# Attention scores by 64x64 matmuls on the four quarters of the array, two units at a time

## The chip, the cores and the metric

One core of one Trainium2 chip runs the whole program in one launch. Its engines are TensorE (PE: matmuls; PEld: its loads of weights), VectorE (DVE), ScalarE (ACT), GpSimd (POOL) and SyncE (SP), which issues most DMAs. The metric is the device time of one execution in microseconds, as the median of several runs.

## What is computed

Three layers, one after another, all in float32 accuracy. Only the first is touched:

```python
scores = scale * np.matmul(q, k.transpose(0, 1, 3, 2))   # q, k, v: 4 x 8 heads x 576 x 64
rel = pos[:, None] - pos[None, :]
mask = (rel >= 0) & (rel < 64)                           # causal, a window of 64
scores = np.where(mask, scores, -1e9)
attn = softmax(scores); x = np.matmul(attn, v)
```

The second layer is `h = x @ w_in`, a rational function of `h`, and `@ w_out` (512 to 2048 to 512, for 2304 tokens). The third sends each token to one of eight experts (512 to 1024 to 512) and scales what comes back.

## The kernel before

The 2304 tokens are cut into nine blocks of 256 (`TB`), and a block's attention into four units, each a pair of heads: 36 units (`NUNIT`), number `n` = 4 u + c. A block holds four pieces of 64 queries (`W`); a piece of queries sees its own 64 keys and the 64 before them, so its scores are 64 x 128 for each head.

A unit goes through four steps. `at_T(n)` turns q and k by four transposes into the PSUM tile `tq`; ScalarE or VectorE copies k's half into `kT[c]` and q's half, scaled, in two copies of 64 x 256 into `qbd`, a tile cleared once in which each piece has the two heads on the diagonal. `at_QK(n)` makes the scores: one matmul for each piece, contracting 128 rows (two heads of 64) and giving 128 rows (head, query) by 128 keys in the tile `sc`, one PSUM bank. VectorE adds the mask and takes the least value, ScalarE the exponential, and the rows are divided by their sums; all four pieces are in the tile `ms`. `at_PT(n)` turns `ms` into PSUM (`pp`) and back. `at_PV(n)` multiplies by v: matmuls of 128 rows by 64 columns, the two heads on the two column halves of the array, into `xp`; from block 3 (`NG`) on it takes two units at once.

An fp32 matmul is two records in the trace, one of fp32r (`h`, `y`, `lt`) is one.

The second layer runs in steps `s` of one block and two pieces of `w_in`; `h` is its first product (each 24 matmuls of 128x128 by 256), `y` its second (12 by 512, four steps later). The attention's work is cut into half-steps (`evs`, two for each unit) and dealt out between those steps by `pace(s)`, which has a block's attention done (`need`) when the second layer comes to it. `ORDER` gives the order of every engine's work in the first twelve steps (`S_TAPE`) by hand, with the units 0 to 12 in it; instructions from there bear the line L125 in the trace. What follows is placed by a planner and bears the line L97. `in_turn` keeps a group of matmuls behind the last such group. The weights are split into high and low parts in the start (`convert`, VectorE's tile `cp`).

Of the kernel before, what the change touches and what calls it, by code (L numbers as in the profile page):

```python
# [23 lines left out]
NQ, TA, VU = 2, 2, 2  # L24
# [107 lines left out]
def kernel(  # L132
# [56 lines left out]
    sizes = dict(cs=C_QC + 1, mb=128, co=6, OH=2 * E, idt=3 * NTILE, npre=E, pre=2 * NPRE, ei=2 * (NSLOT + 1), nsl=1,  # L189
                 CNT=E, CN2=E, tri=64, one=64, sg=24, qbd=NQ * 512, kT=NP * (W + TB))  # L190
# [14 lines left out]
    qbd = [cols["qbd"][:, i * 512:(i + 1) * 512].rearrange("p (b q) -> p b q", b=4) for i in range(NQ)]  # L205
# [197 lines left out]
    def at_T(n):  # L403
        nc.mark()
        u, c = divmod(n, NP)
        tq = pt([128, 2, 2, 128], "tq")
        cc = 2 * (c % 2)
        for a, src in ((0, k_t[n // 2]), (1, q_t[n // 2])):
            for r in range(2):
                nc.tensor.transpose(tq[:, a, r, :], src[:, r, cc:cc + 2, :].rearrange("p h d -> p (h d)"), ident)  # L410
        if u:
            e = pick(D=dve(W, True), A=act(W), G=0.2)
            nc.either(e if e == "G" else "D", G=lambda: nc.gpsimd.tensor_copy(out=kT[c][:, :W], in_=kT[c][:, TB:]),
                      D=lambda: nc.vector.tensor_copy(out=kT[c][:, :W], in_=kT[c][:, TB:]))
        evac(kT[c][:, W:], tq[:, 0].rearrange("d r p -> d (r p)"), TB)
        for hh in range(2):
            lo = 64 * hh
            evac(qbd[n % NQ][lo:lo + 64, :, lo:lo + 64],
                 tq[lo:lo + 64, 1].rearrange("d r (b p) -> d (r b) p", b=2), 256, -scale)

    def spans(nk):
        a = 0
        while a < 4:
            b = a
            while b < 4 and nk[b] == nk[a]:
                b += 1
            yield a, b, nk[a]
            a = b

    def mask(u, i, w):  # L430
        m = mb if u and (4 * u + i) % BPS == 0 else cs[:, C_MASK:C_MASK + 128]
        return m[:, 128 - w:]

    def at_QK(n):
        nc.mark()
        u, c = divmod(n, NP)
        sc = pt([128, 4, 128], "sc")
        ms = t2([128, 4, 128], "ms")
        mn = sm.tile([128, 4], F32, tag="mn", name="mn")
        rs = sm.tile([128, 4], F32, tag="sg", name="rs")  # L440
        nk = []
        kt = kT[c]
        for i in range(4):
            w = W if u + i == 0 else 2 * W
            mm(sc[:, i, :w], qbd[n % NQ][:, i, :], kt[:, i * W + 2 * W - w:(i + 2) * W], True, True)
            nk.append(w)
        for i in range(4):
            charge("D", dve(128))
            nc.vector.tensor_tensor_reduce(
                out=ms[:, i, :nk[i]], in0=sc[:, i, :nk[i]], in1=mask(u, i, nk[i]),  # L450
                scale=1.0, scalar=3.0e38, op0=ALU.add, op1=ALU.min, accum_out=mn[:, i:i + 1],
            )
        for i in range(4):
            charge("A", act(128))
            nc.scalar.activation(out=ms[:, i, :nk[i]], in_=ms[:, i, :nk[i]], func=AF.Exp,
                                 scale=-1.0, bias=mn[:, i:i + 1], accum_out=sg[n % 3][:, i, 0:1])
# [3 lines left out]
        for a, b, w in spans(nk):  # L460
            arith(ms[:, a:b, :w], ms[:, a:b, :w], bc(rs[:, a:b], [128, b - a, w]), ALU.mult, (b - a) * w)
        P_t[n] = (ms, nk)

    def at_PT(n):
        nc.mark()
        ms, nk = P_t.pop(n)
        pp = pt([128, 4, 128], "pp")
        pT = ms
        for i in range(4):
            nc.tensor.transpose(pp[:nk[i], i, :], ms[:, i, :nk[i]], ident)  # L470
        for a, b, w in spans(nk):
            evac(pT[:w, a:b], pp[:w, a:b], (b - a) * 128)
        pT_t[n] = (pT, nk)

    def at_PV(n):
        nc.mark()
        u, c = divmod(n, NP)
        m = 1 if u < NG else 2
        vt = v_t[n // 2]
        xp = pt([128, m, TB], "xp")  # L480
        with in_turn():
            for x in range(m):
                c1 = c - m + 1 + x
                pT, nk = pT_t.pop(u * NP + c1)
                for i in range(4):
                    for hh in range(2):
                        mm(xp[64 * hh:64 * hh + 64, x, i * W:(i + 1) * W],
                           vt[:nk[i], i, 2 * (c1 % 2) + hh, :], pT[:nk[i], i, 64 * hh:64 * hh + 64], True, True)
# [571 lines left out]
    for n in range(NUNIT + 2):  # L1060
        first, second = [], []
        if n < NUNIT:
# [3 lines left out]
        while done < NUNIT and done <= n - 1:  # L1066
            first.append((at_PT, done))
            if done // NP < NG or done % 2:
                second.append((at_PV, done))
            done += 1  # L1070
        evs += [first, second]
# [31 lines left out]
    for t in qbd:  # L1103
        nc.gpsimd.memset(t, 0.0)
    nc.gpsimd.memset(mb[:, :W], BIG)
    nc.gpsimd.tensor_copy(out=mb[:, W:], in_=cs[:, C_MASK + W:C_MASK + 2 * W])
# [218 lines left out]
```

## Time and profile before

| | us |
|---|---|
| median of 3 runs (775.21 to 776.25) | 775.79 |
| the profiled execution | 778.31 |
| its span, first to last instruction | 776.6 |

| engine | busy us | share of the span |
|---|---|---|
| TensorE, matmuls | 749.8 | 97% |
| TensorE, loads of weights | 664.1 | 86% |
| VectorE | 512.5 | 66% |
| ScalarE | 479.3 | 62% |
| GpSimd | 435.6 | 56% |

A record of TensorE lasts from its start until its result is through; records overlap, so the time that one adds to a stream is read from the starts of two groups that follow each other, and not from its duration. The DMA share can pass 1 where packets of several queues overlap. All 16 DMA engines moved 78.53 MB, over a quarter of it in the first 85 us.

### The profile page before, as it was taken

How to read it: one execution, taken by the hardware profiler on the slowest of the kernel's cores; microseconds unless marked ns; L12 is line 12 of the kernel's file. 1: busy time of each engine (PE TensorE's matmuls, PEld its weight loads, DVE VectorE, ACT ScalarE, POOL GpSimd, SP SyncE). 2: the span in 40 equal slices, each digit the busy share in tenths (PEclk: the TensorE clock that was granted, in tenths of full speed). 3: DMA queues.
4: the chain of work that ended last, by engine and by line, in shares of the span. 5: the costliest groups of instructions: out<-in, count | busy, mean ns of one | idle time of the engine just before them, and what ended most of it. 6: DMA issues, size and time to landing. Idle time of an engine off the chain costs nothing. (4 is left out here: it accounts for less than half of the span.)

```text
span 776.6 us, 14180 instructions
## 1 busy us (share of the span) xinstructions
PE 749.8 (97%) x5072; PEld 664.1 (86%) x5072; DVE 512.5 (66%) x1264; ACT 479.3 (62%) x1063; POOL 435.6 (56%) x386
## 2 busy tenths in 40 slices
PE   5798999999999999999999999999999999999996
PEld 4696898999989899999999999897788888888896
DVE  4996999976877767777776776789847423315020
ACT  4997886997766677677668565576552433425131
POOL 3576786765555655564555554576552736354341
PEclk9798999999999999999999999999999999999999
DMA  9999201432221122131131001135605644511610
GB/s 230 304 236 325 66 28 60 145 86 59 69 77 47 28 47 59 28 81 30 28 83 28 1 29 30 53 112 161 215 31 202 220 148 145 167 68 30 220 37 32
DMA packets 96656, 78.53 MB, mean 101 GB/s; under 512 B 74623, under 2 KB 75007, under 8 KB 96576
## 3 DMA queue, kind: packets, MB, share of 16 engines
q1 hardware_dynamic: 92736, 67.77, 30.1%
q0 software_dynamic: 3840, 9.76, 3.8%
q8 instruction: 42, 0.69, 0.4%
q14 instruction: 38, 0.31, 0.1%
HBM read 66.25 MB, written 11.53 MB: 100 GB/s over the span
## 5 line engine op out<-in xcount | busy, mean ns | idle before, releaser
L97 PE MATMUL y<-wo,g 128*128 128x512 f32 x768 | 192.2, 398 | 0.3 <-POOL g L97 0.3
L97 PE MATMUL h<-xh,wi 128*128 128x256 f32 x896 | 171.6, 284 | 0.0
L97 PEld LDWEIGHTS y<-wo,g 128*128 128x128 f32 x768 | 139.2, 188 | 28.4 <-POOL g L97 0.7
L97 PEld LDWEIGHTS h<-xh,wi 128*128 128x128 f32 x896 | 143.7, 191 | 2.3
L97 PE MATMUL h<-xl,wi 128*128 128x256 f32 x448 | 127.8, 285 | 0.0
L97 POOL TENSOR_TENSOR wx<-wr,wx 128x1024 fp32r<-128x1024 f32 x29 | 73.7, 2550 | 50.1 <-ACT wx L97 41.8
L97 PE MATMUL yp<-wx,hT 128*128 128x512 f32 x432 | 99.5, 390 | 0.0
L97 POOL TENSOR_TENSOR g<-t,g 128x512 fp32r<-128x512 f32 x61 | 80.0, 1312 | 33.5 <-ACT g L97 33.0
L97 PEld LDWEIGHTS yp<-wx,hT 128*128 128x128 f32 x432 | 80.7, 188 | 16.5
L97 PEld LDWEIGHTS h<-xl,wi 128*128 128x128 f32 x448 | 85.7, 191 | 2.4
L97 POOL TENSOR_TENSOR qm<-qm,e 128x512 f32<-128x512 f32 x57 | 74.0, 1298 | 24.2 <-ACT qm L97 20.1
L97 ACT ACTIVATE e<-h 128x512 f32<-128x512 f32 x60 | 35.9, 599 | 82.3 <-PE h L97 70.0
L97 PE MATMUL hp<-xbh,wx 128*128 128x512 f32 x256 | 80.2, 391 | 0.0
L97 DVE SCALAR_TENSOR_TENSOR t<-t,KK,r 128x512 f32<-128x512 f32 x61 | 45.3, 743 | 42.4 <-ACT r L97 42.1
L97 DVE SCALAR_TENSOR_TENSOR hT<-hp,hT 128x512 fp32r<-128x512 f32 x36 | 24.6, 687 | 67.2 <-ACT hT L97 67.2
L97 POOL TENSOR_SCALAR qm<-e,KK 128x512 f32<-128x512 f32 x38 | 29.4, 774 | 57.9 <-ACT e L97 52.2
L97 PEld LDWEIGHTS hp<-xbh,wx 128*128 128x128 f32 x256 | 48.1, 188 | 9.9
L97 ACT ACTIVATE r<-qm,KK 128x512 f32<-128x512 f32 x61 | 42.0, 689 | 23.3 <-POOL qm L97 15.4
L97 ACT ACTIVATE ob<-yp,tl 128x512 f32<-128x512 f32 x19 | 13.1, 690 | 69.1 <-PE yp L97 69.1
L97 ACT CAST wx<-wr 128x1024 fp32r<-128x1024 f32 x44 | 44.8, 1046 | 13.4 <-PE hp L97 8.9
L97 POOL DMA_INDIRECT out_dram<-ob,tl x19 | 19.7, 1037 | 54.5 <-ACT ob L97 41.4
L97 PE MATMUL hp<-xbl,wx 128*128 128x512 f32 x128 | 50.0, 390 | 0.0
(223 smaller groups left out, 1649.4 us busy)
## 6 DMA issues: line engine op xcount, KB each, us to landing
wr<-in_moe_w_dram SPq DMA_DIRECT2D x48, 512.0 KB, 4.3
stg<-in_moe_w_in_dram SPq DMA_DIRECT2D x8, 1024.0 KB, 7.2
stg<-in_moe_w_out_dram SPq DMA_DIRECT2D x8, 1024.0 KB, 7.3
v<-in_v_dram SPq DMA_DIRECT2D x58, 128.0 KB, 3.0
q<-in_q_dram SPq DMA_DIRECT2D x32, 128.0 KB, 2.7
k<-in_k_dram SPq DMA_DIRECT2D x32, 128.0 KB, 3.0
y_dram<-ysb SPq DMA_DIRECT2D x12, 256.0 KB, 4.2
yp_dram<-yq SPq DMA_DIRECT2D x6, 256.0 KB, 3.2
```

The costliest lines, as they stand in the source:

```text
L97: return f(*a, **k)
```

## The change

The scores are made by matmuls of 64x64. Of each unit, each head (64 rows of the array) and each of two neighbouring pieces (64 columns) has its own quarter, and each head its own PSUM bank, `sc[hh]`. A unit has eight such matmuls, each of 128 keys. q stays as it comes from the transpose, in `qT` (four buffers in place of two), so it leaves PSUM by one copy of 128 x 256 and no tile has to be cleared for it; the rows of the scores are now (piece, query) of one head instead of (head, query) of one piece, which changes the mask's columns, the place of P in `pT` and the names of the loops, not their counts. Block 0's first piece, which had 64 keys, now has 128, of which the mask takes away the first 64; the fronts of `kT` are set to zero for it.

From block 3 on (`group(n)` = 2) the scores of two units are made together, at the second's turn, 16 matmuls in a row; the transposes of both P follow one unit later, and their values one unit after that, so a block's attention is done two half-steps later. The scores are now under `in_turn`. `ORDER` is made anew: 658 entries in place of 692, with unit 12's scores no longer in it.

```diff
-NQ, TA, VU = 2, 2, 2
+NQ, TA, VU = 4, 2, 2
...
-        for hh in range(2):
-            lo = 64 * hh
-            evac(qbd[n % NQ][lo:lo + 64, :, lo:lo + 64],
-                 tq[lo:lo + 64, 1].rearrange("d r (b p) -> d (r b) p", b=2), 256, -scale)
+        evac(qT[n % NQ], tq[:, 1].rearrange("d r p -> d (r p)"), TB, -scale)
...
+    def group(n):
+        return 1 if n // NP < NG else 2
...
     def at_QK(n):
         nc.mark()
         u, c = divmod(n, NP)
-        sc = pt([128, 4, 128], "sc")
-        ms = t2([128, 4, 128], "ms")
...
-        for i in range(4):
-            w = W if u + i == 0 else 2 * W
-            mm(sc[:, i, :w], qbd[n % NQ][:, i, :], kt[:, i * W + 2 * W - w:(i + 2) * W], True, True)
-            nk.append(w)
+        m = group(n)
+        sc = [pt([128, 2 * m, 2 * W], "sc") for _ in range(2)]
+        with in_turn():
+            for x in range(m):
+                for j in range(2):
+                    for hh in range(2):
+                        for t in range(2):
+                            i, lo = 2 * j + t, 64 * hh
+                            mm(sc[hh][W * t:W * t + W, 2 * x + j, :],
+                               qT[(n - m + 1 + x) % NQ][lo:lo + 64, i * W:(i + 1) * W],
+                               kT[c - m + 1 + x][lo:lo + 64, i * W:(i + 2) * W], True, True)
+        for x in range(m):
+            soften(n - m + 1 + x, [sc[g % 2][:, 2 * x + g // 2, :] for g in range(4)])
...
     def at_PV(n):
...
-                    for hh in range(2):
-                        mm(xp[64 * hh:64 * hh + 64, x, i * W:(i + 1) * W],
-                           vt[:nk[i], i, 2 * (c1 % 2) + hh, :], pT[:nk[i], i, 64 * hh:64 * hh + 64], True, True)
+                    for hh in range(2):
+                        mm(xp[64 * hh:64 * hh + 64, x, i * W:(i + 1) * W], vt[:, i, 2 * ((c - m + 1 + x) % 2) + hh, :],
+                           pT[:, 2 * (i // 2) + hh, W * (i % 2):W * (i % 2) + W], True, True)
...
-        if n < NUNIT:
+        if n < NUNIT and (group(n) == 1 or n % 2):
             first.append((at_QK, n))
         if n + TA < NUNIT:
             second.append((at_T, n + TA))
-        while done < NUNIT and done <= n - 1:
+        while done < min(n, NUNIT) and (group(done) == 1 or n % 2 == 0):
             first.append((at_PT, done))
-            if done // NP < NG or done % 2:
+            if group(done) == 1:
                 second.append((at_PV, done))
             done += 1
+        if n % 2 and n > 2 and group(n - 2) == 2:
+            second.append((at_PV, n - 2))
...
-    for t in qbd:
-        nc.gpsimd.memset(t, 0.0)
-    nc.gpsimd.memset(mb[:, :W], BIG)
-    nc.gpsimd.tensor_copy(out=mb[:, W:], in_=cs[:, C_MASK + W:C_MASK + 2 * W])
+    nc.gpsimd.memset(cols["kT"].rearrange("p (c t) -> p c t", c=NP)[:, :, :W], 0.0)
+    for t in range(2):
+        nc.gpsimd.tensor_copy(out=mb[:, 2 * W * t:2 * W * (t + 1)], in_=cs[:, C_MASK:C_MASK + 2 * W])
+        nc.gpsimd.memset(mb[64 * t:64 * t + 64, 2 * W * t:2 * W * t + W], BIG)
```

(`soften` is the softmax that stood in `at_QK`, over the four score tiles it is given.)

## Rows read from the trace of the kernel before

**Rows 1.** the page's busy times: us, share of the span, instructions, for each engine

```profile
PE 749.8 (97%) x5072; PEld 664.1 (86%) x5072; DVE 512.5 (66%) x1264; ACT 479.3 (62%) x1063; POOL 435.6 (56%) x386
```

**Rows 2.** busy time by stretch: length, busy us (instructions) per engine, granted clock, DMA

```profile
0.00:85.00 85.00, 66.47 (x553) 59.12 (x553) 67.03 (x221) 67.49 (x207) 52.20 (x74) 0.90 0.97 265
85.00:140.00 55.00, 55.00 (x365) 49.90 (x364) 54.77 (x98) 41.83 (x79) 40.16 (x33) 1.00 0.11 39
140.00:455.00 315.00, 314.93 (x2446) 287.41 (x2445) 233.04 (x633) 228.57 (x561) 184.27 (x171) 1.00 0.21 54
```

**Rows 3.** all waits of TensorE: who waited for whom, us in total, times, longest

```profile
PE tq L125 <- DMA KK<-in_const_dram: 7.4, 1, 7.4
PE lt L97 <- DVE yl L97: 1.8, 1, 1.8
```

**Rows 4.** busy time by stretch of the instructions on tile sc alone

```profile
0.00:85.00 85.00, 17.04 (x109) 15.51 (x109) 11.31 (x48) 0.90 0.97 265
140.00:455.00 315.00, 26.04 (x176) 23.04 (x176) 21.56 (x92) 1.00 0.21 54
```

**Rows 5.** TensorE's groups by shape: weights, moving, count; busy us, mean ns

```profile
L97 PE MATMUL h<-xh,wi 128*128 128x256 f32 x896 | 171.6, 284 | 0.0
L97 PE MATMUL sc<-KK 128*128 128x128 f32 x184 | 27.1, 278 | 0.0
L97 PE MATMUL xp<-ms,v 128*64 128x64 f32 x384 | 14.4, 226 | 0.0
L97 PE MATMUL lt<-yh,wg 128*32 128x128 f32 x72 | 12.7, 238 | 0.0
```

**Rows 6.** timeline of TensorE at 84 us: start, us, what, count

```profile
84.55 1.06 PE L97 MATMUL sc<-KK 128*128 128x128 f32 x8
85.45 0.60 PE L125 MATMUL pp<-KK,ms 128*128 128x128 f32 x4
```

**Rows 7.** timeline of TensorE around two groups of xp

```profile
299.73 0.38 PE L97 MATMUL tq<-KK,k 128*128 128x128 f32 x2
299.95 0.38 PE L97 MATMUL tq<-KK,q 128*128 128x128 f32 x2
300.26 1.15 PE L97 MATMUL xp<-ms,v 128*64 128x64 f32 x32
301.35 0.66 PE L97 MATMUL ytp<-KK,ysb 128*128 128x128 f32 x4
...
89.17 0.69 PE L125 MATMUL xp<-ms,v 128*64 128x64 f32 x16
89.78 0.39 PE L125 MATMUL h<-xh,wi 128*128 128x256 f32 x1
```

**Rows 8.** timeline at block 0's xp; two looks cut at 24.645 and 24.66 us

```profile
18.39 0.83 PE L125 MATMUL xp<-ms,v 64*64 64x64 f32 x16
19.15 0.63 PE L125 MATMUL pp<-KK,ms 128*64 128x128 f32 x4
...
24.64 0.24 PE L125 MATMUL xp<-ms,v 64*64 64x64 f32 x1 [1.09 <-ACT ms L125]
24.64 0.27 PE L125 MATMUL xp<-ms,v 64*64 64x64 f32 x2 [1.09 <-ACT ms L125]
```

**Rows 9.** copies from tile tq: count, ns min/median/max, first and last start, shape

```profile
L125 ACT ACTIVATE KK<-tq x26: 372/382/393, 9.5 to 91.6; 64x256 f32<-64x256 f32 x26
L125 ACT COPY KK<-tq x13: 351/374/400, 8.6 to 91.0; 128x256 f32<-128x256 f32 x13
```

**Rows 10.** busy time in stretches of 5 us

```profile
30.00:35.00 5.00, 3.22 (x26) 2.51 (x25) 4.96 (x18) 4.89 (x17) 3.53 (x4) 0.50 0.97 227
65.00:70.00 5.00, 2.63 (x26) 2.03 (x28) 0.66 (x2) 4.78 (x16) 3.94 (x6) 0.90 0.94 227
70.00:75.00 5.00, 4.42 (x18) 3.36 (x15) 4.55 (x12) 1.54 (x3) 1.23 (x2) 0.50 1.05 406
```

**Rows 11.** waits of all engines from 0 to 92 us

```profile
DVE xl L125 <- ACT wo L125: 4.8, 1, 4.8
```

More of the change, by code (lines that the diff above doesn't have):

```diff
@@ L187 @@
     t_dram = dram.tile([E * NT + 2 * TB, 3], U32, name="t_dram")
-    sizes = dict(cs=C_QC + 1, mb=128, co=6, OH=2 * E, idt=3 * NTILE, npre=E, pre=2 * NPRE, ei=2 * (NSLOT + 1), nsl=1,
-                 CNT=E, CN2=E, tri=64, one=64, sg=24, qbd=NQ * 512, kT=NP * (W + TB))
+    sizes = dict(cs=C_QC + 1, mb=256, co=6, OH=2 * E, idt=3 * NTILE, npre=E, pre=2 * NPRE, ei=2 * (NSLOT + 1), nsl=1,
+                 CNT=E, CN2=E, tri=64, one=64, sg=24, qT=NQ * TB, kT=NP * (W + TB))
     tot = sum(sizes.values())
@@ L204 @@
     tri, one = cols["tri"].bitcast(BF16), cols["one"].bitcast(BF16)
-    qbd = [cols["qbd"][:, i * 512:(i + 1) * 512].rearrange("p (b q) -> p b q", b=4) for i in range(NQ)]
+    qT = [cols["qT"][:, i * TB:(i + 1) * TB] for i in range(NQ)]
     kT = [cols["kT"][:, i * (W + TB):(i + 1) * (W + TB)] for i in range(NP)]
@@ L415, in at_T, with mask @@
         evac(kT[c][:, W:], tq[:, 0].rearrange("d r p -> d (r p)"), TB)
-        for hh in range(2):
-            lo = 64 * hh
-            evac(qbd[n % NQ][lo:lo + 64, :, lo:lo + 64],
-                 tq[lo:lo + 64, 1].rearrange("d r (b p) -> d (r b) p", b=2), 256, -scale)
[L421 to L432, printed above, removed]
+        evac(qT[n % NQ], tq[:, 1].rearrange("d r p -> d (r p)"), TB, -scale)
+    def mask(u, j):
+        i = 4 * u + 2 * j
+        if i % BPS == 0:
+            return mb[:, :2 * W]
+        if (i + 1) % BPS == 0:
+            return mb[:, 2 * W:]
+        return cs[:, C_MASK:C_MASK + 2 * W]
+    def group(n):
+        return 1 if n // NP < NG else 2
     def at_QK(n):
@@ L436, in at_QK, with soften @@
         u, c = divmod(n, NP)
-        sc = pt([128, 4, 128], "sc")
-        ms = t2([128, 4, 128], "ms")
+        m = group(n)
[11 more added lines that the diff above has]
+            soften(n - m + 1 + x, [sc[g % 2][:, 2 * x + g // 2, :] for g in range(4)])
+    def soften(n, sc):
+        u, c = divmod(n, NP)
+        ms = t2([128, 4, 2 * W], "ms")
         mn = sm.tile([128, 4], F32, tag="mn", name="mn")
         rs = sm.tile([128, 4], F32, tag="sg", name="rs")
-        nk = []
-        kt = kT[c]
-        for i in range(4):
-            w = W if u + i == 0 else 2 * W
-            mm(sc[:, i, :w], qbd[n % NQ][:, i, :], kt[:, i * W + 2 * W - w:(i + 2) * W], True, True)
-            nk.append(w)
-        for i in range(4):
+        for g in range(4):
             charge("D", dve(128))
             nc.vector.tensor_tensor_reduce(
-                out=ms[:, i, :nk[i]], in0=sc[:, i, :nk[i]], in1=mask(u, i, nk[i]),
-                scale=1.0, scalar=3.0e38, op0=ALU.add, op1=ALU.min, accum_out=mn[:, i:i + 1],
+                out=ms[:, g, :], in0=sc[g], in1=mask(u, g // 2),
+                scale=1.0, scalar=3.0e38, op0=ALU.add, op1=ALU.min, accum_out=mn[:, g:g + 1],
             )
-        for i in range(4):
+        for g in range(4):
             charge("A", act(128))
-            nc.scalar.activation(out=ms[:, i, :nk[i]], in_=ms[:, i, :nk[i]], func=AF.Exp,
-                                 scale=-1.0, bias=mn[:, i:i + 1], accum_out=sg[n % 3][:, i, 0:1])
+            nc.scalar.activation(out=ms[:, g, :], in_=ms[:, g, :], func=AF.Exp,
+                                 scale=-1.0, bias=mn[:, g:g + 1], accum_out=sg[n % 3][:, g, 0:1])
         charge("D", 0.2)
@@ L459, in at_QK @@
         nc.vector.reciprocal(out=rs, in_=rs)
-        for a, b, w in spans(nk):
-            arith(ms[:, a:b, :w], ms[:, a:b, :w], bc(rs[:, a:b], [128, b - a, w]), ALU.mult, (b - a) * w)
-        P_t[n] = (ms, nk)
+        arith(ms, ms, bc(rs, [128, 4, 2 * W]), ALU.mult, 512)
+        P_t[n] = ms
     def at_PT(n):
         nc.mark()
-        ms, nk = P_t.pop(n)
+        ms = P_t.pop(n)
         pp = pt([128, 4, 128], "pp")
[L468 to L473, printed above, removed]
+        for g in range(4):
+            transpose(pp[:, g, :], ms[:, g, :])
+        evac(ms, pp, 512)
+        pT_t[n] = ms
     def at_PV(n):
@@ L477, in at_PV @@
         u, c = divmod(n, NP)
-        m = 1 if u < NG else 2
+        m = group(n)
         vt = v_t[n // 2]
@@ L482, in at_PV @@
             for x in range(m):
-                c1 = c - m + 1 + x
-                pT, nk = pT_t.pop(u * NP + c1)
+                pT = pT_t.pop(n - m + 1 + x)
                 for i in range(4):
                     for hh in range(2):
-                        mm(xp[64 * hh:64 * hh + 64, x, i * W:(i + 1) * W],
-                           vt[:nk[i], i, 2 * (c1 % 2) + hh, :], pT[:nk[i], i, 64 * hh:64 * hh + 64], True, True)
+                        mm(xp[64 * hh:64 * hh + 64, x, i * W:(i + 1) * W], vt[:, i, 2 * ((c - m + 1 + x) % 2) + hh, :],
+                           pT[:, 2 * (i // 2) + hh, W * (i % 2):W * (i % 2) + W], True, True)
         if c == m - 1:
```

66 rows, old and new, of the table ORDER are left out of this document.

## The prediction

> **What bounds the kernel now.** I read the page's busy times first: TensorE is busy for 749.8 us of a span of 776.6 [rows 1]; VectorE and ScalarE have a third to spare. A mean hides stages, so the second view is the busy time by stretch [rows 2]. From 140 to 455 us TensorE is busy for 314.93 of 315 us while VectorE has 233; from 85 to 140 both are full (55.00 and 54.77 of 55); from 0 to 85 TensorE has 66.47 of 85, at a mean granted clock of 0.90, while the DMA share is 0.97. The third view, TensorE's waits, says the same: the waits stand in the code of the first steps (L125), and outside it the longest is one of 1.8 us [rows 3]. So after 85 us a microsecond taken from TensorE is a microsecond off the end; before 85 us it is not, unless what holds TensorE up moves too.
>
> Where do the scores lie? The tile sc takes 17.04 us of TensorE before 85 us and 26.04 us between 140 and 455 [rows 4]: 176 records there, eight a unit, so 22 units, and one more stands at 84.55 us. The other 13 units are in the start. Four matmuls a unit give eight records, so one fp32 matmul is two records.
>
> **What a unit's scores cost now.** The eight records begin at 84.55 and the next work at 85.45 us [rows 6]: 0.90 us, 0.112 a record. Two units: 1.80 us.
>
> **What a group costs after.** Per unit eight matmuls of 64x64 replace four of 128x128, sixteen records for eight, each still streaming 128 columns; they go round four quarters, so two units are 32 records, eight rounds of four. What is a round worth? Quarters aren't in this trace; the nearest rows are the values' matmuls, xp, on the two column halves. There 32 records run from 300.26 to 301.35 us and 16 from 89.17 to 89.78 [rows 7]. The difference is 0.48 us for 16 records, 0.030 each, 0.060 for two: two at a time. That two halves do run at once is seen at block 0: the second record begins within 0.02 us of the first [rows 8], where on the whole array the next begins 0.112 later.
>
> Is a round 0.112 us, as the sc record is now, or less? A record on the whole array loads 128 columns of weights and streams 128 columns; the quarter loads 64 and streams 128, so it matters which of the two sets the 0.112. The durations say streaming: an fp32r record of 128 columns (lt) takes 238 ns and one of 256 (h) 284, an fp32 record of 64 (xp) 226 and one of 128 (sc) 278 [rows 5]. An fp32 column counts as two. So I take 0.112 for a round, with 0.060 (the xp round) as the lower bound; the upper, if two halves of the rows take turns, is 0.224.
>
> A change of the array's layout costs time too. Before xp the step from tq is 0.31 us where two tq records took 0.22 [rows 7]: 0.09 more than one record's pace. Leaving: 32 records at 0.030 explain 0.96 of the 1.09 us, so 0.13. From the 64-row layout to the 128-row one inside block 0: 16 records from 18.39 to 19.15 us [rows 8], 0.76 against 0.61, 0.15 more. A score group thus pays 0.22 for coming and going, the xp price; scores before were on the whole array like their neighbours and paid nothing.
>
> Group of two: 8 x 0.112 + 0.22 = 1.12 us, against 1.80: 0.68 saved. Twelve groups (block 3 on) lie after about 84 us, where TensorE is the bound: **12 x 0.68 = 8.2 us off the end.** A unit alone (blocks 0 to 2): 4 x 0.112 + 0.22 = 0.67 against 0.90, 0.23 saved, twelve times, 2.8 us; all in the start, where I count it only with the rest below.
>
> **The start.** There the ScalarE and VectorE are nearly full early on (4.89 and 4.96 of 5 from 30 to 35 us) and ScalarE still from 65 to 70 (4.78), where VectorE has only 0.66 [rows 10]: VectorE's xl waits 4.8 us for ScalarE [rows 11]. The change takes work from just these: q's transpose leaves PSUM in one copy of 128x256 instead of two of 64x256. Fifteen units' transposes stand in the written-out order, so thirty such halves, 26 of them on ScalarE at 382 ns, and a 128x256 copy takes 374 [rows 9]: fifteen instructions fewer, 15 x 0.38 = 5.7 us. Shared by two engines that are full that is 2.9 us; block 0's split sums go as well. Unit 12's softmax leaves the written-out order, since its scores wait for unit 13. Against it stand a DMA share of 0.97 up to 85 us [rows 2], which this change doesn't touch, and an order made anew, whose stalls nobody can read from this trace. I take **2 us off**, between 6 off (all 5.7 on the path) and 4 on (nearly another stall of the kind that xl had).
>
> **Edits that I cost at nothing.** GpSimd's two big clears of qbd become one smaller one of kT's front columns, and one more mask is copied and filled; these lie before the first scores, beside the wait for the constants' DMA (7.4 us on TensorE [rows 3]). Block 0 now scores 128 columns in place of 64, four reductions and exponentials a little longer. The softmax, the transposes of P, the number of xp records and all DMAs stay, so no queue of SP changes its content, only its place in the new order. Two banks per score group instead of one: eight reductions in place of four hold them; VectorE has 26% to spare from 140 us on, which covers it. If that cover is gone, TensorE waits for a bank: 0 to 1.8 us, the longest such wait outside the start [rows 3]. The scores of the first unit of a pair, and both values, come one unit later; so for blocks from 3 on attention must run two half-steps further ahead. For block 3 that moves about one unit's softmax into or towards 85 to 140 us, where VectorE is full: 0 to 2 us, taken as nothing because TensorE lost nothing there so far.
>
> **Sum.** 8.2 + 2 = 10.2 us. The profiled execution took 778.31 us around its span of 776.6 and would take 768.1; the median of the runs is 775.79 and becomes **765.6 us**. If the start gives nothing, 767.6; with its bounds 761.6 to 771.6.
>
> **Rivals.** (A) is the forecast, chance 0.62.
>
> (B) The start gives the gain back: order made anew, TensorE shorter of work there, one more idle stretch in which the granted clock falls. From 70 to 75 us TensorE was granted 0.50, 1.2 GHz, right after the stretch from 65 to 70 in which it was busy for 2.63 of 5 us [rows 10]. Price 4 to 8 us, so 770 to 776, about 773. For it: 85 us of the span aren't TensorE's. Against: less work for both full engines. Chance 0.15.
>
> (C) Slower: only two of the four quarters run at a time. The place is each group, the price 16 x 0.112 + 0.22 = 2.01 against 1.80 us, +0.21 twelve times, 2.5 us; and the same in twelve units of the start, of which half counts, 1.3. If the start has no relief either, because the longer groups eat it, 775.8 + 3.8 = 779.6; it ranges over 776 to 781. It decides from a round of 0.197 us on ((1.80 - 0.22) / 8). For it: rows of the trace show column halves at once, never row halves. Against: xp at 0.030 a record, and the two heads write different banks. Here too belongs that the change doesn't do what it says: with no overlap at all 32 x 0.112 + 0.22 = 3.80 a group, +24 us, which the xp rows make very unlikely. Chance 0.13.
> The Trainium skill, "TensorE: Matmul & The Clock Gate", Part 3, under what overlaps and what doesn't, has matmuls start and end strictly in the order of the program; an fp32 matmul's second record on the same quarter would then hold up all quarters behind it, each matmul would add a whole round, and the group would cost what (C) says. The trace is against such a rule as far as it goes: block 0's second record begins within 0.02 us of the first [rows 8]; but no run so far has quarters.
>
> (D) A round is set by the weights, 64 columns, as in xp: 8 x 0.060 + 0.22 = 0.70, 1.10 saved, 13.2 us, with the start 760.6. Against: the durations above [rows 5]. Chance 0.10.
>
> **Range and chances.** A spans 761.6 to 771.6, D reaches 759, the better half of B ends near 775. 759 to 775 leaves out C, the rest of B and D's tail, under 0.2. A measurement of this kernel can tell about 0.2% (1.6 us) from no change. Faster: A, D and 0.09 of B: 0.81. Same: 0.04 of B and 0.02 of C: 0.06. Slower: 0.11 of C and 0.02 of B: 0.13.
>
> **What would show it.** In the trace after: a group of 32 sc records whose begin lies about 1.1 us before the next work (0.9 within it); if it is 2.0, (C), if 0.7, (D). The stretch in which TensorE is full should hold about 8 us less. The start: TensorE's solid run, which now begins at about 80 us, should begin at 78; if it begins later than 84, (B). ScalarE's copies from tq should be 128x256, about 36 for q. TensorE's waits after 85 us should stay under 2 us in all; a new wait there for a bank or for q's copy would prove the nothings wrong.

## The result, and the profile after

| | before | after |
|---|---|---|
| median us, runs of one comparison | 776.02 (775.21 to 778.09, 4 runs) | 766.86 (764.19 to 767.84, 4 runs) |
| ratio, 95% interval | 1 | 0.9872 [0.9841, 0.9904] |
| the profiled execution | 778.31 | 766.85 |
| its span | 776.6 | 765.1 |

The forecast was 765.6 us in a range of 759 to 775. The time is right to 1.3 us, but two of the terms behind it are not: the start gave far more than I put down, and the end, where I had put nothing, took some of it back. In what follows lines of the changed kernel bear L123 in the first steps and L95 behind them (L125 and L97 before).

First the page's busy times of the changed kernel, then its busy time by stretch (columns as in [rows 2]):

```profile
PE 737.2 (96%) x5360; PEld 646.7 (85%) x5360; DVE 505.1 (66%) x1264; ACT 467.1 (61%) x1035; POOL 426.9 (56%) x371
...
0.00:85.00 85.00, 68.74 (x712) 58.88 (x713) 72.33 (x231) 68.59 (x207) 56.28 (x70) 0.92 0.93 253
85.00:140.00 55.00, 53.84 (x363) 48.52 (x362) 54.87 (x102) 41.40 (x81) 38.02 (x32) 1.00 0.20 70
140.00:455.00 315.00, 315.00 (x2669) 284.33 (x2668) 233.62 (x649) 224.55 (x543) 182.48 (x168) 1.00 0.21 54
```

TensorE has 288 records more than in [rows 1] and is busy 12.6 us less. From 140 to 455 us it is full as before. What is new stands in its waits behind 85 us (who waited for whom, us in total, times, longest), where [rows 3] have one of 1.8 us:

```profile
PE yp L95 <- DVE hT L95: 2.2, 1, 2.2
PE hp L95 <- DVE xbl L95: 1.9, 1, 1.9
PE h L95 <- DVE t L95: 1.2, 1, 1.2
PE rp L95 <- DVE ob L95: 0.3, 1, 0.3
```

The scores, by form (records, shortest, median and longest ns, first and last start), and one group of two units in the timeline (start us, us, what); they answer to [rows 5] and [rows 6]:

```profile
L95 PE MATMUL sc<-KK x384: 267/269/320, 128.6 to 425.1; 64*64 64x128 f32 x192
...
312.52 0.28 PE L95 MATMUL h<-xh,wi 128*128 128x256 f32 x1
312.73 1.11 PE L95 MATMUL sc<-KK 64*64 64x128 f32 x32
313.77 0.24 PE L95 MATMUL lg<-KK,ls 32*128 32x32 f32 x1
```

From the group's start to the next work is 1.04 us. It starts 0.21 us behind the last record of h, whose pace is 0.12, so coming costs 0.09 more: 1.13 us for two units, where I had worked out 1.12. The ten groups from unit 16 on, between 175 and 425 us, all have this length.

**Where the time went.** To place the gain I compared the start of the same record in both traces: the n-th record of h is the same work in both (both have 1728), though the other work done by then can differ. Differences in us, after minus before:

| record | start before | difference | what lies in between |
|---|---|---|---|
| h, 97th | 59.98 | -0.17 | the first 60 us |
| h, 193rd | 98.38 | -9.16 | the rest of the start; 1.78 of it only moved: units 12 and 13 (16 records at 83.66 before) now come at 128.6 and 132.6 |
| h, 481st | 172.63 | -6.92 | units 12 to 15, and the wait of h for t |
| h, 1633rd | 510.52 | -13.72 | ten groups |
| h, 1728th | 533.99 | -15.64 | the end of the second layer, without the wait of lt for yl [rows 3] |
| yp, last | 770.08 | -11.45 | the experts |

So the start gave 9.16 - 1.78 = 7.4 us, units 12 to 15 lost 7.38 - 6.92 = 0.5, ten groups gave 13.72 - 6.92 = 6.8, and behind the 1633rd record 2.3 were lost: 1.9 came with the wait of lt for yl (1.8 us before) that is gone, and the experts lost 4.2. In sum 7.4 - 0.5 + 6.8 - 2.3 = 11.4, the difference of the two profiled executions. Four transposes of unit 15 (0.45 us at the pace of [rows 7]) lie before the 193rd record in the changed kernel and behind it before, so the start gave that much more, and units 12 to 15 lost that much more. The medians lie 9.2 apart, since the profiled execution of before was 2.3 us above its median and that of after was at its own. Before has one trace only, so where its 2.3 us lie stays open; a figure against the kernel before, such as the 7.4, may hold some of them, while the difference of two kernels that both stand against this trace does not.

### The profile page after: what moved, and what is told of

Its sections match the earlier page's. It is cut to its first block, busy times and chain, and to the rows that moved or that the text cites. A ratio compares the mean times of both kernels' runs of the same rounds, so it can differ in the third digit from the quotient of the medians.

```text
span 765.1 us, 14765 instructions
## 1 busy us (share of the span) xinstructions
PE 737.2 (96%) x5360; PEld 646.7 (85%) x5360; DVE 505.1 (66%) x1264; ACT 467.1 (61%) x1035; POOL 426.9 (56%) x371
## 5 line engine op out<-in xcount | busy, mean ns | idle before, releaser
L95 PE MATMUL y<-wo,g 128*128 128x512 f32 x768 | 191.9, 397 | 0.0
L95 PE MATMUL h<-xh,wi 128*128 128x256 f32 x896 | 172.0, 284 | 1.2 <-DVE t L95 1.2
L95 PEld LDWEIGHTS y<-wo,g 128*128 128x128 f32 x768 | 139.4, 188 | 27.8 <-issue 0.7
L95 PEld LDWEIGHTS h<-xh,wi 128*128 128x128 f32 x896 | 143.7, 191 | 3.7 <-issue 1.5
L95 PE MATMUL h<-xl,wi 128*128 128x256 f32 x448 | 127.9, 285 | 0.0
L95 POOL TENSOR_TENSOR g<-t,g 128x512 fp32r<-128x512 f32 x62 | 80.2, 1293 | 52.2 <-ACT g L95 46.5
L95 PE MATMUL yp<-wx,hT 128*128 128x512 f32 x432 | 100.0, 391 | 2.2 <-DVE hT L95 2.2
L95 POOL TENSOR_TENSOR wx<-wr,wx 128x1024 fp32r<-128x1024 f32 x29 | 72.2, 2506 | 45.5 <-ACT wx L95 37.7
L95 PEld LDWEIGHTS yp<-wx,hT 128*128 128x128 f32 x432 | 80.5, 188 | 19.2 <-DVE hT L95 2.8
L95 POOL TENSOR_TENSOR qm<-qm,e 128x512 f32<-128x512 f32 x56 | 72.5, 1295 | 27.1 <-ACT qm L95 24.7
L95 PEld LDWEIGHTS h<-xl,wi 128*128 128x128 f32 x448 | 85.7, 191 | 2.3
L95 PE MATMUL hp<-xbh,wx 128*128 128x512 f32 x256 | 80.0, 390 | 0.0
L95 DVE SCALAR_TENSOR_TENSOR t<-t,KK,r 128x512 f32<-128x512 f32 x61 | 45.5, 747 | 50.1 <-ACT r L95 49.3
L95 DVE SCALAR_TENSOR_TENSOR hT<-hp,hT 128x512 fp32r<-128x512 f32 x36 | 24.4, 688 | 68.5 <-ACT hT L95 62.2
L95 ACT ACTIVATE e<-h 128x512 f32<-128x512 f32 x60 | 35.6, 594 | 54.6 <-PE h L95 40.2
L95 ACT ACTIVATE r<-qm,KK 128x512 f32<-128x512 f32 x61 | 42.1, 690 | 36.1 <-POOL qm L95 32.7
L95 DVE TENSOR_TENSOR t<-t,h 128x512 f32<-128x512 f32 x60 | 41.0, 683 | 27.6 <-ACT t L95 25.8
L95 ACT ACTIVATE ob<-yp,tl 128x512 f32<-128x512 f32 x19 | 13.0, 689 | 71.1 <-PE yp L95 64.2
L95 PEld LDWEIGHTS hp<-xbh,wx 128*128 128x128 f32 x256 | 48.0, 188 | 9.9
L95 ACT CAST g<-t 128x512 fp32r<-128x512 f32 x62 | 38.3, 618 | 27.3 <-PE h L95 9.8
L95 ACT CAST wx<-wr 128x1024 fp32r<-128x1024 f32 x44 | 44.8, 1047 | 15.7 <-PE hp L95 11.4
L95 PE MATMUL hp<-xbl,wx 128*128 128x512 f32 x128 | 50.2, 392 | 1.9 <-DVE xbl L95 1.9
```

The source lines that it names most:

```text
L95: return f(*a, **k)
```

## The experiments

Three questions: what a group costs and why some don't cost 1.13; what made the start so much shorter; what was lost at the end. Ratios are to the kernel before, with 95% intervals.

### The groups: head_by_head, one_unit, pinned

In the changed kernel the matmuls of a group go round the quarters as the code has them only from unit 16 on. The timeline shows units 12 and 13:

```profile
128.62 1.10 PE L95 MATMUL sc<-KK 64*64 64x128 f32 x16
129.65 3.01 PE L95 MATMUL y<-wo,g 128*128 128x512 f32 x12
132.59 1.10 PE L95 MATMUL sc<-KK 64*64 64x128 f32 x16
133.62 0.62 PE L95 MATMUL h<-x,wi 128*128 128x256 f32 x3
```

Twice 16 records in place of 32: the planner gave first all matmuls of head 0 (two quarters), and those of head 1 behind twelve of y. Each half takes 1.03 us to the next work, as long as a whole group. Units 14 and 15 stand in one run of 32, also head by head, and take 1.53. That is rival (C)'s case in the same trace.

**head_by_head** makes all groups of two units behind the first steps so, with each matmul kept behind the one before it (the edit in short):

```diff
-            for x in range(m): for j in range(2): for hh in range(2):
+            for hh in range(2): for x in range(m): for j in range(2):      # in groups of two units
...
-                mm(sc[hh][...], ...)
+                with behind(x + j + hh + t == 0):      # tc.issue_after(the matmul before), but for the first
+                    mm(sc[hh][...], ...)
```

> The changed kernel, with each group of two units outside the written-out order issuing all of head 0's matmuls and then all of head 1's, so that only two quarters, those of one head, can run at a time. Theory, the four quarters run at once in the changed kernel: each of the ten later groups grows from 1.04 us by seven or eight rounds of 0.118 to about 1.9, ten times 0.83, 8 us in all, 775 us. Rival, the four quarters were not all at work (a round is set by something else): the groups stay near 1.04 and the time at 767.

Measured 772.33 us (768.53 to 776.11), ratio 0.9950 [0.9929, 0.9972], by the medians 5.5 us longer than the changed kernel. Its profiled execution, 768.92, is near its fastest and 2.1 longer. There it stands 8.20 us ahead of the kernel before at the 1633rd record of h, the changed kernel 13.72: 5.5 are lost by then, and the experts give 3.5 of it back, for a reason told below. A group in its timeline:

```profile
342.88 0.28 PE L95 MATMUL h<-xh,wi 128*128 128x256 f32 x1
343.08 1.60 PE L95 MATMUL sc<-KK 64*64 64x128 f32 x32
344.62 0.74 PE L95 MATMUL y<-wo,g 128*128 128x512 f32 x2
```

1.53 us to the next work, 0.49 more than round the quarters; ten groups make 4.9. So the quarters do work four at a time, and the order in which the matmuls are given decides it. My figure for two at a time was too high: the records' starts (ns from the group's first) show why.

```
 0 7 | 160 167 | 272 278 | 383 390 |
 492 498 504* 511* | 600 607 664 671 | 712 718 776 782 | 823 830 887 895 |
 996 1003 | 1104 1112 | 1216 1220 | 1327 1333
```

The two marked records last 320 ns, as the first four of a group in the changed kernel do, and most others 267 to 270; by this, and by the count of 16 records for each head, they are head 1's first. In the program they stand behind all 16 records of head 0, and yet they start when six of these are still to come. Two quarters work alone for four rounds, four together for four, two alone for four.

**pinned** keeps the round of the quarters as the code has it, by the same `behind`, and changes nothing else.

> The changed kernel, with each score matmul behind the one before it in its group outside the written-out order. In the changed kernel the groups of units 12 to 15 have all of head 0's matmuls first and head 1's behind, and take 1.03 + 1.03 and 1.53 us where the ten later ones take 1.04. Theory, only two quarters ran in those: with the quarters in turn again, except for the first two matmuls that come before the second bank is free, each of the two groups takes about 1.6 us with its changes of layout, 0.7 us less in all, 766.2 us. Rival, something else holds these two groups up (a bank, the copies): they stay at 2.2 and 1.7 us.

Measured 764.54 us (762.14 to 766.56), 0.9861 [0.9843, 0.9879]. Units 12 and 13 now:

```profile
128.42 0.44 PE L95 MATMUL sc<-KK 64*64 64x128 f32 x4
128.79 3.02 PE L95 MATMUL y<-wo,g 128*128 128x512 f32 x12
131.74 1.10 PE L95 MATMUL sc<-KK 64*64 64x128 f32 x28
```

The first two matmuls go, the other fourteen follow behind y, in 0.37 and 1.03 us instead of 1.03 twice. At the 385th record of h it stands 8.20 us ahead of the kernel before, the changed one 6.99: 1.2 gained, 0.66 by these lengths (2 x 1.03 - 0.37 - 1.03) and 0.4 in the wait of h for t (0.8 instead of 1.2). Units 14 and 15 go the same way, in 0.37 and 1.03 us instead of 1.53. That the planner held head 1's matmuls back for its PSUM bank, which the first head's doesn't need, fits both kernels but wasn't tested by itself.

**one_unit** scores units 14 to 35 one by one, in the pinned order.

```diff
-        m = group(n)
+        m = group(n) if n < 14 else 1
...
-        if n < NUNIT and (group(n) == 1 or n % 2):
+        if n < NUNIT and (group(n) == 1 or n >= 14 or n % 2):
```

> The kernel pinned, with the scores of one unit at a time from unit 14 on (eight matmuls in place of sixteen); all else stays in pairs. Theory, a change of the array's layout costs about 0.29 us for coming and going (0.09 to enter, 0.20 from the last record's begin to the next work): two groups of one unit take 2 x (0.40 + 0.20) us where one of two takes 1.04, and enter once more, 0.25 us for each pair, eleven pairs, 2.7 us on pinned's 764.5, so 767. Rival, the change is hidden beside other records: 764 to 765.

Measured 766.66 us (766.33 to 769.66), 0.9885 [0.9863, 0.9907], 2.1 above pinned. A unit alone takes 0.60 us to the next work, and 0.09 to come in. The difference of two units and one, 1.04 - 0.60 = 0.44 for four rounds, is the cleanest price of a round: **0.110 us**; what is left, 1.13 - 8 x 0.110 = **0.25**, is the layout change in and out. By it eleven pairs would cost 2.7 us more one by one; the medians show 2.1, with overlapping ranges. The traces show more, 5.2 us at the 1633rd record of h (14.83 ahead of the kernel before in pinned, 9.67 here): units 15, 16 and 18 come split again, into 4 and 12 records, and other work of TensorE moved. So the 0.110 is measured on single groups, and the 0.25 is not confirmed by a time.

### The start: old_order, new_order_old_scores, new_order_unit12_early, two_copies

In [rows 10] VectorE has 0.66 us of work between 65 and 70 us, since it waits for ScalarE [rows 11]. In the changed kernel that hole is gone (columns as in [rows 10]):

```profile
65.00:70.00 5.00, 4.85 (x41) 4.29 (x42) 5.00 (x19) 5.00 (x13) 3.80 (x5) 1.00 1.09 332
70.00:75.00 5.00, 5.00 (x34) 4.39 (x32) 5.00 (x11) 4.97 (x15) 4.19 (x4) 1.00 1.19 275
```

The hole took clock as well as time: before, TensorE was granted 0.50 (1.2 GHz) from 70 to 75 us, behind the stretch in which it was busy for 2.63 of 5 [rows 10], and the first twelve matmuls of y took 5.28 us there. In the changed kernel they take 2.99, at 1.00, which it has in every stretch of 5 us from 40 to 100 us:

```profile
70.93 5.28 PE L125 MATMUL y<-wo,g 128*128 128x512 f32 x12 [0.58 <-DVE xl L125]
...
66.18 2.99 PE L123 MATMUL y<-wo,g 128*128 128x512 f32 x12
```

So up to 2.3 us of the start's gain are clock; no run takes clock and waiting apart. By the table most of the gain lies here, between the 97th and the 193rd record of h.

Is it the new order, the new scores, or the shorter copies? **old_order** is the changed kernel with `ORDER` of before, each entry put to the same piece of work, but for unit 11's scores, which come later.

> The changed kernel with the first twelve steps in the order of the kernel before, each step kept at its place and on its engine; what no longer exists drops out, and unit 11's scores come behind unit 9's values, since two banks per score don't fit beside the other tiles at the old place. The trace of the changed kernel runs 9.2 us ahead when the second layer's fifth step begins (98 us), 1.8 of it because units 12 and 13 haven't had their scores yet; so the start gave about 7 us. Theory A, the order made anew gave most of it: this kernel loses 4 to 7 us against the changed one, 771 to 774 us. Theory B, the work taken away gave it (15 copies fewer on ScalarE and VectorE, shorter scores): it loses 0 to 3 us, 767 to 770.

Measured 770.91 us (768.54 to 772.86), 0.9940 [0.9923, 0.9957]. The hole is back, with a wait of VectorE's xl for ScalarE of 5.0 us:

```profile
65.00:70.00 5.00, 3.52 (x28) 2.69 (x28) 0.33 (x1) 3.25 (x12) 2.22 (x2) 0.68 0.70 149
70.00:75.00 5.00, 4.11 (x26) 2.55 (x24) 5.00 (x13) 1.38 (x3) 1.74 (x3) 0.97 1.02 373
```

At the 193rd record of h it is 1.97 us ahead, of which 1.78 is the move of units 12 and 13: all the new work together (scores, copies, clears) gives the start 0.2 us in the old order.

**new_order_old_scores** is the reverse: the kernel before, with the changed kernel's order. Unit 12's scores come last there, when unit 14's q has taken the place of unit 12's, so this unit is scored with the wrong q.

> The kernel before, with 128x128 scores and two copies of q, but its first twelve steps in the order of the changed kernel; the two halves of a copy stand together, and unit 12's scores, which the new order doesn't have, come last. After the start it is the kernel before. Theory A, the order gave the 7 us of the start: this kernel gains 4 to 7 us on the kernel before, 769 to 772 us. Theory B, the work taken away gave it: 774 to 778 us, no faster than before, as the two engines that are full still have all the copies.

Measured 778.82 us (778.41 to 781.71), 1.0041 [1.0028, 1.0054]. There h waits 3.6 us for t, perhaps for unit 12's late scores. In **new_order_unit12_early** these come earlier, just ahead of the second of the two copies of unit 14's q; so one head of unit 12 is still scored with unit 14's q, which the expectation doesn't say.

> As new_order_old_scores (the kernel before, its first twelve steps in the order of the changed kernel), with one correction: there unit 12's scores stood at the very end of the written-out order, behind unit 14's copy of q into the same buffer, so they took unit 14's q and held up the units behind them from 115 us on; here they come before that copy, some twenty places ahead of where unit 14's values of q leave PSUM in the order, and unit 12's softmax follows. The start is read at the begin of the second layer's ninth step. Theory A, the new order alone gives the start's 7 us: 5 to 7 us ahead of the kernel before there, 769 to 771 us. Theory B', order and shorter work are worth something only together (the order was made for the shorter copies and scores): within 2 us of the kernel before, 774 to 778 us.

Measured 777.41 us (775.05 to 780.25), 1.0011 [0.9995, 1.0027]. At the 193rd record of h it is 2.04 ahead, 0.9 of it one unit that moved: 1.1 for the start, and that is lost again behind it.

So neither does it alone. **two_copies** takes from the changed kernel the one thing that I had priced, in the written-out steps only (the edit in short):

```diff
-        evac(qT[n % NQ], tq[:, 1]..., TB, -scale)
+        for z in (0, 64):                       # two instructions on the same engine, in the same place of the order
+            scaled copy of qT[n % NQ][z:z + 64] from tq[z:z + 64, 1]
```

> The changed kernel with its new order untouched; only in the written-out first steps q leaves PSUM by two copies of 64x256 again, one after the other on the same engine, in place of one of 128x256 (about fifteen instructions of 0.38 us more, 5.7 us, on ScalarE and VectorE, which are full there). Theory (the start's gain of about 7 us is the relief of these two engines, which only a new order can use): about half of the added time or more comes back on TensorE's path, 3 to 6 us at the 192nd record of h and 770 to 773 us in all, against 766.9. Rival (the relief doesn't matter; the gain is the shorter matmuls, the shorter list and the order): within 1.5 us of the changed kernel, 766 to 768, and the first h at 34.7 us as there.

Measured 769.08 us (768.09 to 771.67), 0.9913 [0.9898, 0.9929]. Its halves of q by form (thirty for fifteen units; the first steps are L126 here), and its busy times in the same windows:

```profile
L126 ACT ACTIVATE KK<-tq x26: 364/381/396, 13.8 to 85.3; 64x256 f32<-64x256 f32 x26
L126 DVE TENSOR_SCALAR KK<-tq x4: 417/422/428, 9.2 to 10.8; 64x256 f32<-64x256 f32 x4
...
65.00:70.00 5.00, 4.46 (x48) 4.03 (x48) 4.72 (x16) 4.95 (x16) 4.14 (x5) 1.00 1.02 297
70.00:75.00 5.00, 4.48 (x38) 3.91 (x39) 4.95 (x19) 4.94 (x11) 3.26 (x4) 1.00 0.51 158
```

The hole stays closed: that is the order's doing. But ScalarE and VectorE are at 4.7 to 4.95 of 5 and TensorE waits (4.46 and 4.48). At the 193rd record of h it is 2.93 ahead, the changed kernel 9.16: fifteen short copies, 5.7 us of engine time, are **6.2 us of the path**, as much as they take and a little more. (The seven traces with the changed kernel's first steps stand 8.84 to 9.36 ahead there, so 6.2 is far outside their spread.) Of it 5.5 stand already at the 97th record, where two_copies is 5.30 behind the kernel before and the changed kernel 0.17 ahead. From there to the 193rd all three in the new order gain on the kernel before, new_order_unit12_early 6.7, two_copies 8.2 and the changed kernel 9.0, and old_order 1.3. So the new order closes the hole, and with the old copies it pays about 5 us for that in the first 60 us; the short copies take this price away. Without them the start gives 2.93 - 1.78 = 1.1, as in new_order_unit12_early. At the end only 2.3 of the 6.2 are left by the medians (769.08 to 766.81), for a reason that belongs to the next question.

### The end: after_again, split_on_gpsimd, pinned_split

From the 1633rd record of h to the end the changed kernel loses 2.3 us to the one before, while old_order gains 2.0 there, two_copies 1.3 and pinned 1.5. GpSimd's and VectorE's rows of the changed kernel, at the splits of the experts' weights (wx):

```profile
605.12 9.44 POOL L95 TENSOR_TENSOR wx<-wr,wx 128x1024 fp32r<-128x1024 f32 x4
...
607.91 7.74 DVE L95 TENSOR_TENSOR wx<-wr,wx 128x1024 fp32r<-128x1024 f32 x1 [4.16 <-ACT wx L95]
615.57 1.27 DVE L95 SCALAR_TENSOR_TENSOR hT<-hp,hT 128x512 fp32r<-128x512 f32 x2
```

VectorE's subtraction takes 7.74 us, where the median of its fifteen is 1.23. It begins when GpSimd's second of four such subtractions has just begun and ends 1.1 us behind the last of them, at 615.65. Behind it in VectorE's queue stands hT, and for that yp waits 2.2 us. **after_again** asks whether this is the program or one execution.

> The changed kernel once more, word for word, beside the one with two copies. Theory A (VectorE's subtraction of 7.7 us beside GpSimd's four at about 608 us belongs to this program's timing): the profile shows it again, a wait of yp for hT of about 2 us, and a time of 766 to 768 us. Theory B (it fell so in one execution only): the longest such subtraction is 3.3 us, as in the kernels with the matmuls in program order, the wait is gone, the span is 761 to 763 us, and the median is 763 to 765.5 us.

Measured 766.81 us (765.58 to 767.74), 0.9877 [0.9862, 0.9892]. It is there again, with a wait of yp of 2.0:

```profile
603.99 9.46 POOL L95 TENSOR_TENSOR wx<-wr,wx 128x1024 fp32r<-128x1024 f32 x4
...
606.94 7.60 DVE L95 TENSOR_TENSOR wx<-wr,wx 128x1024 fp32r<-128x1024 f32 x1 [4.16 <-ACT wx L95]
```

**split_on_gpsimd** gives this one subtraction to GpSimd:

```diff
-        arith(w[:, 1, :], t, f32(w[:, 0, :]), ALU.subtract, 1024)
+        if (j, x) == (2, 4):
+            charge("D", 3 * dve(1024))                  # the planner's account as before
+            nc.gpsimd.tensor_tensor(out=w[:, 1, :], in0=t, in1=f32(w[:, 0, :]), op=ALU.subtract)
+        else:
+            arith(w[:, 1, :], t, f32(w[:, 0, :]), ALU.subtract, 1024)
```

> The changed kernel, with one weight split of the third expert slot (its fifth of eight) on GpSimd in place of VectorE. In the changed kernel that split takes VectorE 7.74 us where 1.22 is usual, while GpSimd does four splits in a row from 605.1 to 614.6 us; VectorE's hT comes late and TensorE waits 2.2 us at 614. Theory, VectorE's split is held up by GpSimd's: the wait goes, 764.5 us. Rival, TensorE's wait comes from elsewhere (the five splits on GpSimd now late themselves, or hT waits for ScalarE): a wait of 2 us or more stays within 20 us of the place, 766 to 768 us.

Measured 763.63 us (763.17 to 764.11), 0.9846 [0.9834, 0.9859], 3.2 below the changed kernel. VectorE's longest is now 3.26 us and the wait of yp is gone:

```profile
PE h L95 <- DVE t L95: 1.2, 1, 1.2
PE hp L95 <- DVE xbl L95: 0.9, 1, 0.9
PE rp L95 <- DVE ob L95: 0.3, 1, 0.3
...
L95 DVE TENSOR_TENSOR wx<-wr,wx x14: 1220/1225/3264, 536.9 to 736.5; 128x1024 fp32r<-128x1024 f32 x14
```

In pinned, two_copies and head_by_head the same subtraction takes 2.57 or 2.58 us; there the four of GpSimd don't come in one row:

```profile
600.74 2.42 POOL L95 TENSOR_TENSOR wx<-wr,wx 128x1024 fp32r<-128x1024 f32 x1
604.58 8.09 POOL L95 TENSOR_TENSOR wx<-wr,wx 128x1024 fp32r<-128x1024 f32 x3 [1.42 <-ACT wx L95]
...
605.48 2.57 DVE L95 TENSOR_TENSOR wx<-wr,wx 128x1024 fp32r<-128x1024 f32 x1 [4.15 <-ACT wx L95]
```

(These rows are of pinned.) VectorE comes in between two of GpSimd's there. GpSimd's row begins when a DMA that it waits for has ended: 3.80 and 3.96 us before VectorE's subtraction in the two executions of the changed kernel, 5.75 in pinned, 6.26 in head_by_head and 6.86 in two_copies. So the loss hangs on how the two engines meet, and two_copies, which comes 6 us later, was spared it: that is why its end shows so little of what its start lost.

**pinned_split** is both edits together.

> pinned and split_on_gpsimd together. Pinned's trace has no wait of TensorE over 0.8 us after 85 us, so the split has nothing left to give there: 763 to 764.5 us, the same as the better of the two. If the two gains are independent, pinned's 2.3 and the split's 3.2 us, 761.4.

Measured 763.70 us (763.40 to 765.34), 0.9845 [0.9824, 0.9867]: the same as split_on_gpsimd. At the 1633rd record of h it is 1.2 us ahead of that one (14.59 to 13.41), at the last yp 0.4 (15.05 to 14.67); its wait of hp for xbl is 1.6 us instead of 0.9. The medians of both lie about 3.2 us below the changed kernel's and 12 below that of the kernel before.

## Why the prediction was right, and where it was not

**The group's price: right.** 8 rounds of 0.112 and 0.22 for the layout were 1.12; measured 8 x 0.110 + 0.25 = 1.13. The step that carried it was the argument from [rows 5] that the stream, not the load of weights, sets a round. Rival (D) with 0.060 falls by the same number.

**Rival (C): wrong as a rule, right in two places.** Four quarters run at once wherever the matmuls are given round the quarters. Where they were given head by head, two ran at a time: units 12 and 13 took twice 1.03, about the 2.01 of (C) in all. I had read the order of the loops in the code as the order on the engine; behind the written-out steps the planner may change it within a group, and it did in two of twelve.
The rule that I weighed with it, of the Trainium skill, "TensorE: Matmul & The Clock Gate", Part 3, under what overlaps and what doesn't, has matmuls start strictly in the program's order. The traces differ, and they decide: the changed kernel's group takes 1.04 us where I had worked out 2.01 by the rule, and in head_by_head, where all of head 0 stands first, head 1's first records start 504 ns into the group, ahead of six of head 0's.

**Twelve times 0.68 = 8.2: mis-sized.** Ten groups gave 6.8, which is the term. Units 12 to 15, for which it has 1.4, lost 0.5: run by halves, and with a wait of h for t of 1.2 us. I had named a PSUM bank as the cover of two banks per group and looked for a wait there; what came instead was a changed order, which no view of waits shows. My sign, waits of less than 2 us in all after 85 us, failed: they are 5.6, 1.2 here and the rest in the experts.

**The start, 2 us: the term that failed.** It gave 7.4. The 5.7 us of copies were counted rightly, then halved because two engines share them, then cut again for an order that nobody could read. two_copies shows that all of it and a little more (6.2) is path. I read this so that two engines that are full and feed each other are not two lanes that share a load: what one is spared, the other gets earlier. That reading was not tested by itself. The upper end of the bounds, 6 with all of it on the path, was the better reading, and the condition for it was the new order, since all the new work in the old one is worth 0.2. What the order gives in return is the closed hole of [rows 10], its waits and up to 2.3 us of clock, which I had read and had put no gain on. Rival (B), the start gives the gain back, is nearest to new_order_unit12_early: the new order without the relief is no faster than before.

**Edits at nothing: one held, one didn't.** Mask and clears show in no wait of TensorE. A DMA does: a transpose in the start waits 1.9 us for k, and before none waited for k. It stands in old_order too (1.8) and not in two_copies, so it isn't what tells the fast starts from the slow ones. But I followed the path only as far as the second layer. The experts behind it came 13.7 us earlier, into another meeting of VectorE and GpSimd, and of the 4.2 us lost there split_on_gpsimd gets 3.2 back, by the medians.

So 8.2 + 2 = 10.2 stood for 6.3 + 7.4 - 2.3 = 11.4 in the profiled execution. The time was near because the errors were of opposite sign.

## What to carry to other kernels

Give matmuls of different quarters alternately and pin that order: here the same 32 records took 1.04 us round the quarters and 1.53 head by head, and a planner that doesn't know it may undo it. Where two engines are full and wait for each other in turn, price a relief at its whole length, and ask whether the order of the work lets it through: here fifteen copies fewer were worth 6.2 us in the new order, and all the new work together 0.2 in the old. When work comes earlier, follow it to the end of the program: what it meets there can be new.

## What the runs showed of the hardware that I had not expected

**Quarters run ahead of the program's order, but not far.** In head_by_head the other head's matmuls start 0.50 us into the group, when each of the first head's quarters has come to its third matmul of four. How far ahead TensorE looks can't be read from this.

**VectorE can be held for several of GpSimd's instructions in a row.** Its subtraction of 128x1024 takes 1.23 us in the median, took 2.57 when it came 0.90 us into the first of GpSimd's three, and 7.74 and 7.60 when it came into the second of four, ending 1.1 us behind the last. The Trainium skill, "SBUF — State Buffer", under who interferes with whom, says that a VectorE instruction with two inputs in SBUF contends with a GpSimd instruction that reads SBUF, and that the later one is blocked whole; the rows agree, and add that it need not get in between two of them. Why it did in pinned and did not in the changed kernel stays open.
